# Softmax sums and reciprocals moved into earlier pairs of f tiles, and three x loads moved behind the transposes, in a fused dynamic convolution and two-matmul kernel

## The chip, the cores and the metric

The kernel runs on one core of a Trainium2 chip. The metric is the device time of one execution in microseconds (us). Ratios are the mean time of one kernel's fast runs over that of the other's fast runs of the same rounds, so they are not quite the ratio of the medians that are quoted.

Engines in the profile: PE is TensorE's matmuls, PEld its weight loads, DVE is VectorE, ACT is ScalarE, POOL is GpSimd, SP is SyncE, which issues most DMAs.

## The reference, cut to what matters

```python
def _attn_ref(x, weight_gen):                     # x (8, 4096, 192), weight_gen (8, 4096, 8, 7)
    w = softmax(weight_gen, axis=-1)              # exp, sum over 7 taps, divide
    # out[b, s, h, g] = sum over k of w[b, s, h, k] * x_pad[b, s + k, h, g]   (7 taps, causal)
    ...
def _moe_ref(x, w_in, w_out):                     # 32768 tokens, 192 -> 2048 -> 192
    h = x @ w_in
    g = h - np.tanh(h)
    return (g @ w_out).astype(np.float32)
```

## The kernel before

The 32,768 tokens are cut into 32 superblocks n of 1,024 tokens. A superblock goes through these stages:

* SyncE loads x and the tap weights. ScalarE takes the exp; VectorE takes sums, reciprocals and the scaled weights (`softmax_norm`).
* GpSimd multiplies x by the seven taps (`products`), two superblocks ahead of TensorE's use.
* TensorE adds up the taps and transposes in one go, by matmuls with an identity (`conv`); ScalarE copies the result out of PSUM (`convT`).
* TensorE's first matmul makes 16 f tiles (`gemm1`); for each, ScalarE takes the tanh and VectorE subtracts (`gt`). TensorE's second matmul (`gemm2`) runs a superblock behind, a block of tokens per pair p of f tiles.

All instructions stand in the order in which the program writes them. The parts that the change touches:

```python
psum_h = ...tile_pool(name="psum_h", bufs=3, PSUM)      # three tiles rotate: ph of gemm1, pc of conv

def softmax_norm(n, bank):
    wsm = wgpool.tile([P, J, H, K], FP32, name="wsm")
    zr_v = bank[:, 512 - J * H : 512]
    nc.vector.tensor_copy(zr_v, zr_of[n][:])            # reciprocals into PSUM, beside the transposes
    scale(nc.vector, wsm[:], e_of[n], zr_v)             # reads them there
    ...
for n in range(NTOT):
    if n + 3 < NTOT:
        load_x(n + 3)                                   # waits for GpSimd to be done with x of n + 1
    for p in range(J):
        gemm1(n, 2 * p); gemm1(n, 2 * p + 1)
        ...
        if n + 3 < NTOT:
            if p == 1:
                softmax_exp(n + 3)
            if p == 1 and n + 4 < NTOT:
                load_wg(n + 4)
            if 2 <= p <= 5:
                softmax_sum(n + 3, (p - 2) * 2, (p - 1) * 2)
            if p == 6:
                softmax_recip(n + 3, 0, J // 2)
        ...
        if p == 6 and n < NTOT - 1: break
    # the end of a superblock: "tail" below
    gemm2((n - 1) * J + 6, between=between)             # with the transposes of the third chunk mixed in
    conv(n + 1, (0, 1))                                 # the other two chunks, back to back
    gemm2((n - 1) * J + 7, 0, FILL)
    if n + 3 < NTOT:
        softmax_recip(n + 3, J // 2, J)
        softmax_norm(n + 3, pcs[0][:, 0])
    gemm1(n, NFT - 2)                                   # f tile 14
    gemm2((n - 1) * J + 7, FILL, HALF)
    gemm1(n, NFT - 1)                                   # f tile 15
    gemm2((n - 1) * J + 7, HALF, NFT)
```

Superblocks 0 to 3 add all seven taps on TensorE (seven groups of transposes). From 4 on, a DMA adds pairs of taps first, and TensorE has fewer transposes.

The softmax here doesn't subtract the row's maximum and nothing guards it: scores larger than these inputs give would overflow.

## Time and profile before

| | before |
|---|---|
| median of 4 runs | 768.27 us (767.70 to 769.29) |
| TensorE busy, profiled execution | 739.1 of 765.5 us |
| superblock in the middle (subtraction to subtraction) | 22.77 us |
| superblocks 1, 2, 3 | 28.30, 23.91, 22.97 us |

A superblock's length is read here from the start of VectorE's first subtraction of one to that of the next. "Hole" means time in which TensorE does nothing although no semaphore holds it: the profile calls its releaser "issue". The profile gives a hole as idle time after the modelled end of the last matmul; counted from record to record, as the prediction and the expectations do, it is some 0.2 us longer. Records are TensorE's instructions in the order in which they start, counted from 0, its sequencer's own included. A "fetch" is a packet of 16 KiB on the instruction queue of the trace; no view lists these singly, their times were read from the trace's DMA packets. The profile's lines themselves are shown in the prediction.

### The profile page before, as it was taken

Reading aid. Unit: us, or ns where it says so; the run is one execution under the profiler, and the core shown is the slowest. Engines: PE = TensorE matmul, PEld = TensorE weight load, DVE = VectorE, ACT = ScalarE, POOL = GpSimd, SP = SyncE. Lnnn points to the kernel's source line nnn. Section 1 sums busy time; section 2 is a strip of 40 time slices with the busy share of each in tenths; the row PEclk is TensorE's granted clock in tenths of the full one; section 3 lists DMA queues with packets and bytes.
Section 4 is the critical chain, followed back from the end, with each engine's and each line's share of the span. In section 5 each row is a group of like instructions: output and inputs, shape, how many; then the busy total and the mean of one; then the engine's idle time right before and its main releaser. Section 6 shows DMA issues by size and latency. Waiting matters only on the chain.

```text
span 765.5 us, 32560 instructions
## 1 busy us (share of the span) xinstructions
PE 739.1 (97%) x14848; PEld 564.6 (74%) x14848; DVE 681.1 (89%) x765; ACT 642.0 (84%) x869; POOL 668.9 (87%) x262
## 2 busy tenths in 40 slices
PE   4798999999999999999999999999999999999997
PEld 2476777777777777777777777777777777777777
DVE  7986899999999999999999999998999999998893
ACT  4886788888888888888888888888888888888882
POOL 8999999999999999999999999999999999999000
PEclk9999999999999999999999999999999999999999
DMA  8911467665555775545775555766555676542312
GB/s 217 236 42 57 134 171 183 182 175 121 124 151 163 182 181 117 130 150 156 182 184 129 131 144 147 182 179 151 133 131 149 173 182 169 118 122 64 81 43 85
DMA packets 25399, 110.04 MB, mean 144 GB/s; under 512 B 4671, under 2 KB 9519, under 8 KB 21294
## 3 DMA queue, kind: packets, MB, share of 16 engines
q1 hardware_dynamic: 14718, 77.03, 29.1%
q0 software_dynamic: 10544, 30.94, 25.5%
q8 instruction: 116, 1.90, 1.0%
q14 instruction: 21, 0.17, 0.1%
HBM read 54.52 MB, written 25.17 MB: 104 GB/s over the span
## 4 chain that ended last, share of the span: by engine, by line
PE 79%; DVE 15%; ACT 3%; issue 1%; DMA 1%; DVEq 0%
PE ph L308 39%; PE obank L342 37%; DVE gt L320 9%; ACT th L319 3%; DVE wsm L193 2%; PE pc L267 2%; DVE zr L163 2%; PE po L377 1%; DMA x_t<-in_x_dram 1%; DVE pc L169 1%; DVE odd L219 0%; DMA wg_t<-in_weight_gen_dram 0%; DVE even L219 0%; DVE zsum L154 0%; DVE obank L193 0%
## 5 line engine op out<-in xcount | busy, mean ns | idle before, releaser
L320 DVE TENSOR_TENSOR gt<-ph,th 128x1024 bf16<-128x1024 f32 x512 | 604.9, 1220 | 62.0 <-ACT th L319 52.8
L319 ACT ACTIVATE th<-ph 128x1024 f32<-128x1024 f32 x512 | 500.3, 1021 | 66.7 <-PE ph L308 64.8
L342 PE MATMUL obank<-w_out,gt 64*128 64x192 bf16 x7936 | 399.9, 243 | 0.8 <-ACT out_sb L361 0.4
L308 PE MATMUL ph<-convT,w_in 64*128 64x512 bf16 x3072 | 384.4, 378 | 7.9 <-DVE gt L320 2.9
L342 PEld LDWEIGHTS <-gt 64*128 64x128 bf16 x7936 | 343.6, 94 | 65.5 <-issue 0.9
L219 POOL TENSOR_TENSOR even<-x_t,wsm 128x1536 bf16<-128x1536 f32 x93 | 272.6, 2931 | 27.5 <-DVE gt L320 27.2
L219 POOL TENSOR_TENSOR odd<-x_t,wsm 128x1536 bf16<-128x1536 f32 x93 | 272.6, 2931 | 0.0
L308 PEld LDWEIGHTS <-w_in 64*128 64x128 bf16 x3072 | 163.6, 94 | 115.6 <-issue 11.7
L219 POOL TENSOR_TENSOR last<-x_t,wsm 128x1536 bf16<-128x1536 f32 x32 | 105.9, 3308 | 0.0
L361 ACT ACTIVATE out_sb<-obank 128x192 f32<-128x192 f32 x248 | 81.6, 329 | 7.0 <-PE obank L342 2.6
L291 ACT ACTIVATE convT<-pc 128x512 bf16<-128x512 f32 (+1 forms) x63 | 50.7, 807 | 30.1 <-PE pc L267 30.1
L267 PE MATMUL pc<-ident,even 64*128 64x64 bf16 x2256 | 56.1, 191 | 0.6 <-issue 0.4
L267 PEld LDWEIGHTS <-even 64*128 64x128 bf16 x2304 | 53.2, 96 | 1.4 <-issue 0.7
L234 POOL DMA_DIRECT2D even<-odd x28 | 33.7, 1205 | 8.7 <-POOL odd L219 8.7
L267 PE MATMUL pc<-ident,last 64*128 64x64 bf16 x752 | 26.8, 192 | 9.4 <-POOL last L219 9.2
L154 DVE TENSOR_REDUCE zsum<-e_t 128x16 f32<-128x112 f32 (+1 forms) x116 | 31.5, 271 | 3.0 <-ACT e_t L143 3.0
L267 PEld LDWEIGHTS <-last 64*128 64x128 bf16 x768 | 19.7, 96 | 9.7 <-POOL last L219 9.2
L143 ACT ACTIVATE e_t<-wg_t 128x448 f32<-128x448 f32 x32 | 18.5, 578 | 6.5 <-DMA wg_t<-in_weight_gen_dram 6.5
L267 PE MATMUL pc<-ident,odd 64*128 64x64 bf16 x464 | 18.5, 198 | 3.7 <-issue 2.6
L193 DVE TENSOR_TENSOR wsm<-e_t,pc 128x448 f32<-128x448 f32 x28 | 17.4, 622 | 3.1 <-DVE pc L169 0.2
L267 PEld LDWEIGHTS <-odd 64*128 64x128 bf16 x512 | 15.1, 100 | 4.6 <-issue 2.7
L163 DVE RECIPROCAL zr<-zsum 128x32 f32<-128x32 f32 (+1 forms) x58 | 16.6, 327 | 0.1
(27 smaller groups left out, 64.5 us busy)
## 6 DMA issues: line engine op xcount, KB each, us to landing
x_t<-in_x_dram SPq DMA_DIRECT2D x31, 1344.0 KB, 9.0
even<-odd POOLq DMA_DIRECT2D x28, 1024.0 KB, 8.8
out_dram<-out_sb SPq DMA_DIRECT2D x31, 768.0 KB, 11.6
wg_t<-in_weight_gen_dram SPq DMA_DIRECT2D x32, 224.0 KB, 7.8
x_t<-in_x_dram SPq DMA_DIRECT2D x1, 768.0 KB
w_out<-in_moe_w_out_dram POOLq DMA_DIRECT2D x1, 768.0 KB, 8.8
out_dram<-out_sb SPq DMA_DIRECT2D x4, 192.0 KB, 1.8
x_t<-in_x_dram SPq DMA_DIRECT2D x1, 504.0 KB
```

The source lines that it names most:

```text
L154: nc.vector.reduce_sum(out=zsum_of[n][:, j0 * H : j1 * H], in_=e_of[n][:, j0:j1].rearrange("p j h k -> p (j h) k"), axis=AX.X,)
L163: nc.vector.reciprocal(zr_of[n][:, j0 * H : j1 * H], zsum_of[n][:, j0 * H : j1 * H])
L193: return eng.tensor_mul(wsm.rearrange("p j h k -> p (j h) k"), e_t[:].rearrange("p j h k -> p (j h) k"), zr.rearrange("p (n o) -> p n o", ...
L219: mul = eng.tensor_mul(dst[k][:, :, j0:j1].rearrange("p c j h g -> p j h c g"), x_t[:, k + j0 : k + j1, :].rearrange("p j (h c g) -> p j h ...
L234: nc.gpsimd.dma_start(out=even[:].rearrange("p i c j h g -> p (i c j h g)")[:, 0:ACC], in_=odd[:].rearrange("p i c j h g -> p (i c j h g)" ...
L267: nc.tensor.matmul(pc[r][:, col : col + R] if home else pc[:, r, col : col + R], lhsT=prods[c][gi][r * R : (r + 1) * R, c, 2 * j : 2 * j + ...
L291: nc.scalar.activation(out=out, in_=pc[:, :, 0:cols].rearrange("p r (cj t) -> p r cj t", t=R), func=ACT.Copy,)
L308: nc.tensor.matmul(ph[:, r, :], lhsT=w_in[r * R : (r + 1) * R, c, f * P : (f + 1) * P], rhs=convT[r * R : (r + 1) * R, c, :], start=(c == ...
L319: last_act[0] = nc.scalar.activation(out=th[:], in_=ph_f, func=ACT.Tanh)
L320: last_sub[0] = nc.vector.tensor_sub(gt[:], ph_f, th[:])
L342: mm = nc.tensor.matmul(po[:, 0:D], lhsT=g_of[n][f][r * R : (r + 1) * R, col : col + P], rhs=w_out[r * R : (r + 1) * R, f, :], start=(r == ...
L361: last_act[0] = nc.scalar.activation(out=out_sb[:, j, :], in_=po[:, 0:D], func=ACT.Copy)
```

## The change

The intent: take the reciprocals off VectorE's row behind f tile 13, where f tile 15 waits for the product; and keep three early x loads out of the transposes.

```diff
@@ the pairs of f tiles
-                if p == 1:
+                if p == 0:
                     softmax_exp(n + 3)
-                if p == 1 and n + 4 < NTOT:
+                if p == 0 and n + 4 < NTOT:
                     load_wg(n + 4)
-                if 2 <= p <= 5:
-                    softmax_sum(n + 3, (p - 2) * 2, (p - 1) * 2)
-                if p == 6:
-                    softmax_recip(n + 3, 0, J // 2)
+                if 1 <= p <= 3:
+                    softmax_sum(n + 3, (p - 1) * 3, min(p * 3, J))
+                if 4 <= p <= 5:
+                    softmax_recip(n + 3, (p - 4) * JH, (p - 3) * JH)
@@ the tail
-            softmax_recip(n + 3, J // 2, J)
             softmax_norm(n + 3, pcs[0][:, 0])
@@ the x loads
+    LATE = (1, 2, 3)
...
-        if n + 3 < NTOT:
+        if n + 3 < NTOT and n not in LATE:
             load_x(n + 3)
...
+        if n in LATE:
+            load_x(n + 3, last_conv[0])      # behind ScalarE's copy of the transposes of n + 1
```

More of the change, by code (lines that the diff above doesn't have):

```diff
@@ L81 @@
     last_exp = {}
+    last_conv = {}
     first_halo = {}
@@ L290, in conv_out @@
             else:
-                nc.scalar.activation(
+                last_conv[0] = nc.scalar.activation(
                     out=out,
```

## The prediction

> **What bounds the kernel now.** I read the page first: engine shares, then the chain that ended last, then the costliest groups.
>
> ```profile
> PE 739.1 (97%) x14848; PEld 564.6 (74%) x14848; DVE 681.1 (89%) x765; ACT 642.0 (84%) x869; POOL 668.9 (87%) x262
> PE 79%; DVE 15%; ACT 3%; issue 1%; DMA 1%; DVEq 0%
> ```
>
> TensorE is the bound: 97% busy and 79% of the chain. Nothing that merely lightens another engine pays; only time in which TensorE stands still or runs slowly can be won. The summary of waits lists the little there is:
>
> ```profile
> PEld L308 <- DVE wsm L193: 8.5, 24, 0.5
> PE pc L267 <- issue: 3.0, 2, 2.6
> ```
>
> The first is a regular wait, 24 times some 0.35 us: first-matmul weights wait for the softmax normalisation. The second is a single hole of 2.6 us in the transposes with no wait behind it. They fit the two parts of the change, so I looked at each.
>
> *The regular wait.* VectorE's timeline at the end of a middle superblock (n = 17), columns start, length, instruction:
>
> ```profile
> 426.84 2.36 DVE L320 TENSOR_TENSOR gt<-ph,th 128x1024 bf16<-128x1024 f32 x2
> 429.12 0.56 DVE L163 RECIPROCAL zr<-zsum 128x32 f32<-128x32 f32 x2
> 429.77 0.23 DVE L169 COPY pc<-zr 128x64 f32<-128x64 f32 x1
> 430.11 0.62 DVE L193 TENSOR_TENSOR wsm<-e_t,pc 128x448 f32<-128x448 f32 x1
> ```
>
> Both reciprocals, the copy and the product stand in a row behind f tile 13. Three PSUM tiles rotate: f tile 15 takes the one that held the last transposes, and the product still reads its reciprocals there until 430.73. In the trace the matmuls ahead of f tile 15 run out so that it could start at 430.48; it starts at 430.79: 0.31 us lost.
>
> *The hole.* TensorE's timeline, and SyncE's issues near it:
>
> ```profile
> 58.82 0.22 PE L267 MATMUL pc<-ident,odd 64*128 64x64 bf16 x3
> 61.65 0.53 PE L267 MATMUL pc<-ident,odd 64*128 64x64 bf16 x13 [2.61 <-issue]
> ```
>
> ```profile
> 33.21 21.39 SPq L110 DMA_DIRECT2D x_t<-in_x_dram  x2
> 59.85 0.73 SPq L120 DMA_DIRECT2D x_t<-zero  x1
> ```
>
> TensorE stops after 3 of 16 like matmuls, so no operand is missing. The second of the two x loads merged in the first SyncE line (x of superblock 4) goes out at about 54.3 us, and the zeroing that must follow its landing is issued at 59.85. The hole lies at that load's end. Windows from f tile 13's subtraction to the next superblock's first one, for n = 1, 2 and 17 (PE, PEld, DVE, ACT, POOL busy; clock; DMA share; GB/s):
>
> ```profile
> 57.29:68.06 10.77, 8.16 (x207) 6.30 (x201) 4.98 (x8) 5.15 (x8) 10.77 (x5) 0.84 0.25 89
> 84.89:91.97 7.08, 6.69 (x203) 5.08 (x196) 4.89 (x9) 5.05 (x8) 7.08 (x3) 1.00 0.02 4
> 427.99:433.93 5.94, 5.81 (x147) 4.26 (x140) 4.98 (x8) 5.04 (x8) 5.64 (x3) 1.00 0.22 41
> ```
>
> n = 1 and 2 transpose seven groups, n = 17 fewer; yet n = 1 takes 3.7 us more than n = 2 for equal work, at a granted clock of 0.84.
>
> **What the Trainium skill says.**
> (1) "Runtime: NRT & Kernel Launch", section Instruction fetch mechanics: an engine's instructions stream in by a DMA queue in blocks of 16 KiB, 256 instructions, normally hidden. The trace agrees on the block (116 packets, 1.90 MB on the instruction queue), not on the hiding: counting TensorE's records, the hole is ahead of record 1,729 and a smaller one (0.55 us at 86.90) ahead of 2,753, just four blocks on. The block before 1,729 was begun at 56.61; the next fetch started only at 59.37, took 0.96, and TensorE resumed 1.32 after that.
> (2) "DMA: Bandwidth & Descriptors", section Queues, rings and completion order: each engine takes turns between queues packet by packet. The trace shows less fairness for this fetch: it began when the x load ended.
> (3) "TensorE: Matmul & The Clock Gate", Part 1: an idle window of some 3.4 us halves the clock. Here the hole is shorter, but the record shows half clock for 3.41 us from 61.3.
> (4) "VectorE: DVE Perf Modes", The TRN2 errata: small instructions carry a fixed cost. It agrees: sums of 112 elements take 0.26 us, of 448 take 0.62.
>
> **The change, part by part.**
> *Sums and reciprocals earlier.* Before, four sums of 2 j in pairs 2 to 5 and both reciprocals behind f tile 13. After, sums of 3, 3 and 2 j in pairs 1 to 3 and one reciprocal in each of pairs 4 and 5. The line through 0.26 and 0.62 gives 0.32 us for a sum of 3 j. A pair leaves VectorE 0.34 us from a sum's start to the next subtraction (421.27 to 421.61). Instructions overlap by about 0.08, so a sum of 3 j occupies some 0.24 to 0.27 and a reciprocal 0.26 (the second starts 0.26 after the first): all fit, with under 0.1 to spare. Behind f tile 13 the copy then starts at 429.12 and the product ends at 430.08, 0.65 earlier, ahead of 430.48: the wait of 0.31 goes.
> Not all of it is won. The next superblock's second tile needs the PSUM tile of f tile 14, whose subtraction ends at 432.47 whatever the norm does (its tanh waits for ScalarE's copy of the transposes). With release latency 0.05 it can start at 432.52, not at 432.67 - 0.31 = 432.36. So the gain is 432.67 - 432.52 = 0.15. The trace has this experiment already: superblocks 29 and 30 have no softmax left, and ScalarE's big copy of transposes comes 22.64 us after its predecessor (702.72 to 725.36), against 22.77 in the middle: 0.14. I take 25 superblocks (n = 4 to 28) x 0.14 = **3.5 us**.
>
> *Exp and the weight load a pair earlier.* ScalarE's exp (0.58) moves behind f tile 1. Its idle there is about 0.3, and its copy out moves along; I count nothing. In n = 1 two exps meet and VectorE already runs late with the ramp's sum and reciprocal (0.61 + 0.55): I charge **0.25 us**.
>
> *Late x loads.* x of 4, 5, 6 goes out behind the copy of the transposes. In n = 1 the fetch then meets a quiet DMA. Fetch to use still takes 0.1 to 0.4 + 0.95 + 1.35 = about 2.6, and the dense block lasts 2.25 (56.61 to 58.86), so 0.3 of the 2.8 us gap stays: 2.5 won. The half clock goes too: n = 1's tail is 10.77 - 7.08 = 3.7 above n = 2's, whose own hole is 0.55, so 4.2 is hole and clock together, and 4.2 - 2.8 = 1.4 is the clock. n = 2 may win 0.3, n = 3 0.1. Sum 2.5 + 1.4 + 0.4 = **4.3 us**.
> Does GpSimd starve? Its products of 4 start at 75.28; x of 4 would go out near 60.3, and land by 66 to 72 with the zeroing. x of 5: out 84, landed 93, wanted 96.5. x of 6: out 106, landed 115, wanted 118. No.
>
> **The rivals.**
> (a) *The collision moves on.* GpSimd runs back to back until 160 us and sets when the x loads of 7 and 8 go out (118.57 and 140.13), whereas TensorE arrives some 5 us earlier. In n = 4 a fetch asked for near 122 would start when x of 7 ends (124.2), usable at 126.5, wanted at 127.1: just enough. In n = 5 fetches near 140.2 and 147.9 stand against x of 8 and the output at 148.73: a hit costs 1 to 3 us. I charge **0.8 us**; all of it would bring the time to 765.
> (b) *VectorE becomes the bound.* A subtraction must end 0.05 before TensorE wants its tile, and in a pair it has 0.13. If sum or reciprocal overlapped less than I read, 5 pairs x 0.05 x 25 would cost 6 us and eat the gain (767). For it: 89% busy; against it: the ramp, where a subtraction follows a sum 0.21 after its start.
> (c) *The hole isn't the x load's fault* but the density of the transposes. Then n = 1 keeps its 2.8 us and only 3 us are won (766). For it: n = 2's hole at a DMA share of 0.02. Against it: the fetch that started 2.8 us after its block was due, as x ended.
>
> **Range and chances.** 768.7 - 3.5 - 4.3 + 0.25 + 0.8 = 761.9; I say 761.8. Without any new collision and with the holes gone altogether it would be near 760; (a) in full gives 765. So 759.5 to 765.5 for 8 in 10. Two per cent would be 15.4 us, twice the sum of all I can find idle; a loss of 2% needs a new wait of 0.9 us per superblock. Hence 0.01, 0.97, 0.02.
>
> **What would show it.** Right: the wait of weights on the softmax product gone from the list, the subtraction of f tile 14 unmoved relative to the copy, superblocks of 22.63 to 22.64; no hole near 59, no half clock at 61 to 65; x of 4 issued near 60. Wrong: issue holes in n = 4 or 5, matmuls waiting for subtractions in pairs 1 to 5, or a hole that stays at 59.

## The result

The changed kernel takes 763.66 us (median of 4, 762.46 to 765.21) against 768.27 before; the ratio is 0.994 (95% interval 0.9917 to 0.9962). By the 2% mark that is "same", and it is inside the range; but the gain is 4.6 us where 6.5 from this base (6.9 from 768.7) was predicted. The profiled execution is the fastest of the four, 762.46.

The page of the changed kernel (busy time, then the chain that ended last):

```profile
PE 737.8 (97%) x14848; PEld 575.5 (76%) x14848; DVE 676.3 (89%) x737; ACT 642.3 (84%) x869; POOL 668.7 (88%) x262
PE 93%; DVE 4%; DMA 1%; ACT 1%; issue 1%; ACTq 0%; DVEq 0%
```

VectorE's share of the chain falls from 15% to 4%: its row in the tail no longer carries it. VectorE's timeline there (n = 17; start, length, instruction):

```profile
423.16 0.34 DVE L164 RECIPROCAL zr<-zsum 128x32 f32<-128x32 f32 x1
423.50 2.36 DVE L321 TENSOR_TENSOR gt<-ph,th 128x1024 bf16<-128x1024 f32 x2
425.77 0.22 DVE L170 COPY pc<-zr 128x64 f32<-128x64 f32 x1
426.09 0.62 DVE L194 TENSOR_TENSOR wsm<-e_t,pc 128x448 f32<-128x448 f32 x1
427.90 2.38 DVE L321 TENSOR_TENSOR gt<-ph,th 128x1024 bf16<-128x1024 f32 x2 [1.18 <-ACT th L320]
```

The copy now follows the subtractions at once, and VectorE then idles for 1.18 us, because the subtraction of f tile 14 waits for its tanh. The wait of weights on the product is gone from the list of waits; in its place the list has a longer entry without a named releaser:

```profile
PEld L309 <- issue: 19.4, 54, 1.1
PE pc L268 <- issue: 1.4, 3, 0.5
PE obank L344 <- issue: 0.9, 1, 0.9
```

What was added to the first line (11.7 us in 29 times before) is the second tile of a superblock: it has 8.9 us of it in 30 times, and had 1.2 in 4. In the trace its weights start 0.055 us after the subtraction of f tile 14 ends (429.124 and 429.179), so it is this wait although the view names no releaser. The other two lines are holes. TensorE's timeline at three of them, in superblocks 1, 4 and 5:

```profile
59.96 0.36 PE L268 MATMUL pc<-ident,odd 64*128 64x64 bf16 x13 [0.54 <-issue]
...
129.67 0.71 PE L268 MATMUL pc<-ident,even 64*128 64x64 bf16 x37 [0.50 <-issue]
...
154.26 0.26 PE L344 MATMUL obank<-w_out,gt 64*128 64x192 bf16 x2 [0.91 <-issue]
```

The hole near 59 is much shorter (0.73 us from record to record, where it was 2.80) but not gone; superblocks 4 and 5 have holes that the kernel before did not have. The windows of the tails of n = 1, 2, 4, 5 and 17, with the same columns as in the prediction:

```profile
57.66:64.91 7.25, 6.68 (x202) 5.09 (x196) 4.32 (x7) 5.04 (x8) 7.25 (x4) 1.00 0.31 103
81.94:89.04 7.10, 6.68 (x202) 5.07 (x196) 4.32 (x7) 5.04 (x8) 7.10 (x3) 1.00 0.32 105
128.70:134.99 6.29, 5.77 (x142) 4.22 (x136) 4.33 (x7) 5.04 (x8) 6.29 (x3) 1.00 0.13 50
152.02:158.72 6.70, 5.79 (x145) 4.14 (x139) 4.42 (x7) 5.15 (x8) 6.40 (x4) 1.00 0.29 118
424.64:430.27 5.63, 5.63 (x143) 4.18 (x137) 4.34 (x6) 5.04 (x8) 5.33 (x3) 1.00 0.20 38
```

n = 1 falls from 10.77 to 7.25 at full clock; n = 2 keeps its length; 4 and 5 take 0.66 and 1.07 more than n = 17. The ledger of the two profiled executions:

| superblocks | before | after | won |
|---|---|---|---|
| 1 | 28.30 | 25.17 | 3.13 |
| 2 | 23.91 | 24.13 | -0.22 |
| 3 | 22.97 | 22.71 | 0.26 |
| 4 | 22.77 | 23.24 | -0.47 |
| 5 | 22.77 | 23.73 | -0.96 |
| 6 | 22.77 | 22.56 | 0.21 |
| 7 to 28 | 501.34 | 498.35 | 2.99 |
| 29 | 22.47 | 22.64 | -0.17 |

The sum is 4.8 us, which is the difference of the spans (765.5 and 760.7). The single middle superblock is 22.64 us.

### The profile page after: what moved, and what is told of

Its sections match the earlier page's. It is cut to its first block, busy times and chain, and to the rows that moved or that the text cites. A ratio compares the mean times of both kernels' runs of the same rounds, so it can differ in the third digit from the quotient of the medians.

```text
span 760.7 us, 32533 instructions
## 1 busy us (share of the span) xinstructions
PE 737.8 (97%) x14848; PEld 575.5 (76%) x14848; DVE 676.3 (89%) x737; ACT 642.3 (84%) x869; POOL 668.7 (88%) x262
## 3 DMA queue, kind: packets, MB, share of 16 engines
HBM read 54.52 MB, written 25.17 MB: 105 GB/s over the span
## 4 chain that ended last, share of the span: by engine, by line
PE 93%; DVE 4%; DMA 1%; ACT 1%; issue 1%; ACTq 0%; DVEq 0%
PE obank L344 43%; PE ph L309 43%; PE pc L268 6%; DVE gt L321 3%; PE po L379 1%; DMA x_t<-in_x_dram 1%; DVE odd L220 0%; DMA wg_t<-in_weight_gen_dram 0%; DVE even L220 0%; ACT th L320 0%; DVE zsum L155 0%; ACT e_t L144 0%; DVE zr L164 0%; DVE wsm L194 0%; ACT convT L286 0%
## 5 line engine op out<-in xcount | busy, mean ns | idle before, releaser
L309 PE MATMUL ph<-convT,w_in 64*128 64x512 bf16 x3072 | 391.3, 378 | 5.0 <-DVE gt L321 2.7
L344 PEld LDWEIGHTS <-gt 64*128 64x128 bf16 x7936 | 350.0, 94 | 59.6 <-issue 1.1
L309 PEld LDWEIGHTS <-w_in 64*128 64x128 bf16 x3072 | 172.8, 94 | 107.2 <-issue 19.4
L155 DVE TENSOR_REDUCE zsum<-e_t 128x24 f32<-128x168 f32 (+2 forms) x88 | 27.5, 312 | 3.0 <-ACT e_t L144 3.0
L164 DVE RECIPROCAL zr<-zsum 128x32 f32<-128x32 f32 (+1 forms) x58 | 20.3, 350 | 0.1
```

The costliest lines, as they stand in the source:

```text
L155: nc.vector.reduce_sum(out=zsum_of[n][:, j0 * H : j1 * H], in_=e_of[n][:, j0:j1].rearrange("p j h k -> p (j h) k"), axis=AX.X,)
L164: nc.vector.reciprocal(zr_of[n][:, j0 * H : j1 * H], zsum_of[n][:, j0 * H : j1 * H])
L309: nc.tensor.matmul(ph[:, r, :], lhsT=w_in[r * R : (r + 1) * R, c, f * P : (f + 1) * P], rhs=convT[r * R : (r + 1) * R, c, :], start=(c == ...
L344: mm = nc.tensor.matmul(po[:, 0:D], lhsT=g_of[n][f][r * R : (r + 1) * R, col : col + P], rhs=w_out[r * R : (r + 1) * R, f, :], start=(r == ...
```

## The experiments

The theory after the result: (1) the sums and reciprocals win 0.14 us per superblock and no more, because the next wait is close behind. (2) The late loads win the hole and the slow clock of superblock 1. (3) TensorE's instructions come in blocks of 256, and a hole opens where TensorE uses a block faster than the next one is fetched: because the fetch waits behind an x load, or simply because the transposes use instructions so fast. Then late loads only move the collision to the next superblock whose transposes meet a load. The rivals: the holes hang on the transposes or their data; VectorE is the bound in the pairs; the late loads carry all of the gain.

Each kernel ran in 5 rounds beside the kernel before, whose medians in the three calls were 768.59, 768.47 and 768.83 us.

### One part alone: sums_only and late_only

```diff
-    LATE = (1, 2, 3)
+    LATE = ()
```

> The changed kernel with the list of late loads empty: only the sums, reciprocals, exp and weight load moved. My theory: middle superblocks of 22.64 us as in the changed kernel (22.77 before), so some 3.3 us won there; the hole of 2.6 us near 59 us with its stretch of half clock stays, because x of superblock 4 still goes out at 54. Time about 765.0 to 765.5, if the early superblocks lose nothing more. Rival (the late loads are what carries the gain): about 768.

Measured: 766.16 us (764.45 to 766.48), ratio 0.9955 (0.9941 to 0.9969). The middle superblock is 22.64. TensorE's timeline has two large holes:

```profile
61.68 0.36 PE L268 MATMUL pc<-ident,odd 64*128 64x64 bf16 x13 [2.09 <-issue]
...
87.34 0.24 PE L268 MATMUL pc<-ident,even 64*128 64x64 bf16 x5 [2.04 <-issue]
```

The first is the known one (2.28 us from record to record). The second is larger than before (2.23 against 0.55), and here the half clock follows the second (87.82 to 91.23), not the first. So this part alone wins 0.14 us per superblock and makes superblock 2 worse, which I had not expected. TensorE arrives earlier at x of superblock 5: the block ahead of the hole begins at 82.82 instead of 84.06, and the fetch at 85.11, 2.29 after it instead of 0.43.

late_only is the kernel before with the `LATE` lines of the change.

> The kernel before with only the three late x loads. Theory: the hole at 59 shrinks from 2.6 to about 0.7 us and the half clock goes (some 3.3 us won), middle superblocks stay at 22.77; part of that is given back in superblocks 4 and 5, where TensorE now comes earlier than the x loads of 7 and 8 have drained: holes of 0.3 to 1.2 us there. Time about 765.5 to 767. Rival (the collisions at 4 and 5 need both parts): no new hole, 765.

Measured: 765.65 us median of 6, ratio 0.9972 (0.9944 to 0.9999). One of the six took 772.48 and makes the interval wide; five took 764.78 to 767.42. The middle superblock stays at 22.77. The holes from record to record: 0.60 in superblock 1, 1.11 in 2, 0.75 in 4, 0.62 in 5. The collisions in 4 and 5 therefore need only the late loads; the rival is out. Superblock 2 was worse, 1.11 against 0.55.

So each part alone wins 2 to 3 us by the medians, and both together 4.6; neither carries it all.

### Where the collision goes: late_to5

```diff
-    LATE = (1, 2, 3)
+    LATE = (1, 2, 3, 4, 5)
```

> The changed kernel with x of 7 and 8 loaded late as well (superblocks 1 to 5). Theory (the holes of 0.7 us in superblock 4 and 1.2 us in superblock 5 are instruction fetches held up by x of 7 and 8 and what queues behind them): both holes shrink to 0.4 us or less, superblocks 4 and 5 fall from 23.24 and 23.73 towards 22.7, time 1 to 1.5 us below the changed kernel (near 762.4), unless GpSimd then waits for x (wanted at 140 and 161, landing at 139 to 141 and 160 to 162), which would show as a GpSimd wait and cost TensorE nothing. Rival (the holes come from where the 256-instruction blocks end, not from the loads): holes unchanged.

Measured: 764.55 us (763.94 to 764.75), ratio 0.9941 (0.9928 to 0.9954): no gain over the changed kernel. The hole of superblock 4 is gone (none above 0.2) and that of 5 is 0.45, as the theory wants. But two new ones stand in superblocks 6 and 7:

```profile
174.72 0.19 PE L268 MATMUL pc<-ident,odd 64*128 64x64 bf16 x1 [0.37 <-issue]
...
200.47 0.41 PE L268 MATMUL pc<-ident,last 64*128 64x64 bf16 x15 [1.98 <-issue]
```

GpSimd's timeline shows why the second is so large:

```profile
166.67 2.90 POOL L220 TENSOR_TENSOR even<-x_t,wsm 128x1536 bf16<-128x1536 f32 x1 [4.79 <-DVE gt L321]
```

GpSimd stood 4.8 us ahead of superblock 8's products, longer than I expected, so x of 10 went out only at 188.33, and the fetch of the block that begins at 200.47 was 3.41 us late in starting. The subtraction that the view names had long been done (159.73). The trace shows what GpSimd waited for: x of 8, one of the late loads, begins a batch, so the zeroing of its first rows must follow it. That was issued at 159.50, but its six packets of 768 bytes moved only at 165.24 to 165.61, while GpSimd's own DMA that adds the pairs of taps was on its way (159.51 to 166.74); the semaphore that GpSimd's sequencer waited for got its last increment at 166.51. The collision moved on. My expected gain did not come.

### Where the blocks end: shift128, shift128b and shift256

Small matmuls are put ahead of the first transposes, while TensorE idles anyway. They write a PSUM tile that nothing reads; it takes one turn in the rotation of the three, in shift256 as well. Each is two instructions (weight load, matmul), so 64 of them move all later instructions by half a block, and 128 by a whole one.

```diff
+    pad = psum_h.tile([P, 2, HT], FP32, name="pad", tag="ph")
+    for _ in range(64):                                   # shift256: 128
+        nc.tensor.matmul(pad[:, 0, 0:R], lhsT=ident[0:R, :], rhs=ident[0:R, 0:R],
+                         start=True, stop=True)
     conv(0, (0, 1), (2,))
```

> The changed kernel with 64 weight loads and 64 small matmuls into an unused PSUM tile, put ahead of the first transposes while TensorE idles until 9 us: no work on the path, but every later TensorE instruction comes 128 later in its stream, half a block. Theory (a block of 256 instructions is fetched only when the one two before it is used up, so a hole opens where one block is used faster than the 2.9 us that a fetch takes): the holes of 0.73 and 0.58 us in superblocks 1 and 2 go, since there no block lies wholly in dense transposes; time 1 to 2 us below the changed kernel, with holes at other records, each still at a multiple of 256 plus 193. Rival (the holes hang on the transposes or on data): same holes at the same transposes, same time.

Measured: four executions took 762.31 to 763.58 us (ratio 0.992, 0.9906 to 0.9934), but the profiled one took 1,983.28 us and is no use for the holes: TensorE was busy 99% of it, every matmul stretched (832 ns against 378 for the first matmul, 455 against 243 for the second), and the trace has no record of the granted clock. It was not seen again in the other kernels' executions, and its cause stays open.

> The kernel with 64 small matmuls ahead of the first transposes once more: in its first call four executions took 762.3 to 763.6, but the profiled one took 1983 us with every matmul stretched, so its trace tells nothing of the holes. Theory: no hole above 0.3 us in superblocks 1 and 2; what holes there are stand at a record of 193 plus a multiple of 256, now half a block earlier in the kernel's text; about 1 us below the changed kernel of this call. Rival: holes at the same transposes as in the changed kernel.

Measured: 762.05 us (761.72 to 763.25), ratio 0.9922 (0.9908 to 0.9935), against 763.97 and 0.9944 for the changed kernel in the same call. The tails of superblocks 1 and 2 take 6.54 us each (7.25 and 7.10 in the changed kernel): their holes are gone. Only one hole above 0.25 us is left, in superblock 4:

```profile
131.89 0.51 PE L344 MATMUL obank<-w_out,gt 64*128 64x192 bf16 x8 [1.84 <-issue]
```

It stands at TensorE's record 4,801, which is 193 plus 18 x 256, and no longer in the transposes but in the second matmul.

> The changed kernel with 128 small matmuls (256 instructions, one whole block) ahead of the first transposes: as much idle time filled as with 64 and more, but the ends of the blocks fall on the same transposes as without them. Theory (where the blocks end decides): the holes of some 0.7 and 0.6 us in superblocks 1 and 2 are back, at records 1,985 and 3,009, and those of superblocks 4 and 5 too; time as the changed kernel, 763 to 764.5. Rival (the early matmuls help in another way, by warming the clock or by delaying something): no holes in 1 and 2, time near 762.

Measured: 764.40 us (761.72 to 767.50), ratio 0.9936 (0.9915 to 0.9957). The holes are back at the very transposes where the changed kernel has them:

```profile
60.39 0.36 PE L268 MATMUL pc<-ident,odd 64*128 64x64 bf16 x13 [0.89 <-issue]
...
84.69 0.24 PE L268 MATMUL pc<-ident,even 64*128 64x64 bf16 x5 [0.69 <-issue]
```

From record to record they are 1.07 and 0.88 us, even longer than in the changed kernel (0.73 and 0.58): the fetches took 1.40 and 1.22 us here, 0.96 and 0.99 there. Their records are 1,985 and 3,009, and those of superblocks 4 and 5 are 4,801 and 5,825, each one block later than in the changed kernel. As much idle time was filled as with 64 matmuls and more, so it is the place of the block ends that counts. This decides for the instruction blocks. Over 13 profiles (before, after, and all but shift128's stretched one), 46 instructions of TensorE from record 449 on start more than 0.41 us after the one before without waiting for a semaphore, and all 46 stand at a record of 193 plus a multiple of 256. (The limit is just above the 0.40 us of a first matmul at the half clock.) The fetches fit too: all 46 start 1.19 to 1.58 us after a fetch has ended, however late that fetch began (0.06 to 4.55 us after the block before).

### What the fetch waits for: after_x4 and sums_x4, with after_again

```diff
-            dma = rows(0, P)
-            if behind is not None:
-                order(dma, behind, "order of the loads")
+            for r0, r1 in ((0, 4), (4, 8), (8, 11), (11, 14)):
+                dma = rows(0, P, r0, r1)
+                if behind is not None:
+                    order(dma, behind, "order of the loads")
```

after_again is the changed kernel as it is.

> The changed kernel once more, as the measure for the three others of this call. Theory and rival alike: 763 to 764; its holes of about 0.7, 0.6, 0.7 and 1.2 us in superblocks 1, 2, 4 and 5 again, within a few tenths (how far the fetches are held up varies from run to run).

Measured: 763.97 us (762.84 to 765.40), ratio 0.9944 (0.9932 to 0.9957). The holes in its profiled execution (765.40, the slowest of the five) are 0.72, 0.58, 1.11 and 1.97: the first two repeat, those in superblocks 4 and 5 vary by 0.4 and 0.8 from the first profile (0.69 and 1.15). That is much of the spread between executions.

> The changed kernel with each x load issued as four loads of 3 or 4 of its 14 rows. In the profile of the kernel before, the fetch that was late began 0.01 us after the last descriptor of the x load had gone through: 8 descriptors of 10,752 bytes for each DMA engine, one after the other. Theory (an engine finishes the descriptors of one load before it turns to the fetch): with pieces of a quarter, a fetch waits about 1 us instead of 3, so the holes in superblocks 4 and 5 fall below 0.4 us, those of 0.7 and 0.6 in superblocks 1 and 2, which no load causes, stay; time 1 to 1.5 us below the changed kernel. Rival (the fetch waits for everything queued, or for the bandwidth): holes of 4 and 5 unchanged.

Measured: 762.79 us (761.87 to 763.28), ratio 0.9925 (0.9912 to 0.9937). The time is about 1.2 us below the changed kernel, though the intervals overlap a little, and not for the expected reason: its profile (763.28, the slowest of the five) has a hole of 1.92 in superblock 4, a larger one than after_again's. Only that of 5 is small (0.28).

> The changed kernel without its late loads, with each x load in four pieces. Theory: the holes of 2.3 us in superblocks 1 and 2, which the same kernel with whole x loads showed, shrink to about 1 us, and no half clock follows; time near 763.5, so that splitting the load does what delaying it does. Rival (only keeping the load out of the transposes helps): holes above 2 us, time near 766.

Measured: 763.91 us (763.62 to 765.06), ratio 0.9943 (0.9931 to 0.9956).

```profile
61.48 0.36 PE L269 MATMUL pc<-ident,odd 64*128 64x64 bf16 x13 [2.18 <-issue]
```

Superblocks 1 and 2 have holes of 2.37 and 1.90 us, as with whole loads (2.28 and 2.23): **my theory of one load's descriptors is wrong**. In superblock 2 the fetch began at 84.36, after the last packets of x (83.35) and of the tap weights (83.92) and among those of an output (82.40 to 85.77), all issued by 78.9; the smaller loads did not let it in between. What a fetch waits for is not settled by this: in the kernel before, one began at 124.16, with only 48 of the 128 packets of an x load through, and the trace doesn't say which DMA engine moved a packet. That sums_x4 is still some 2 us faster than sums_only fits its clock: no half clock followed its holes. I don't know why, and the two kernels ran on different chips.

### Whether VectorE has room: lumped and one_back

lumped takes the sum in one piece in pair 1 and the reciprocal in one piece in pair 4; one_back leaves the first reciprocal in pair 4 and puts the second behind f tile 13 again.

```diff
 # lumped
-                if 1 <= p <= 3:
-                    softmax_sum(n + 3, (p - 1) * 3, min(p * 3, J))
-                if 4 <= p <= 5:
-                    softmax_recip(n + 3, (p - 4) * JH, (p - 3) * JH)
+                if p == 1:
+                    softmax_sum(n + 3)
+                if p == 4:
+                    softmax_recip(n + 3)
 # one_back
-                if 4 <= p <= 5:
-                    softmax_recip(n + 3, (p - 4) * JH, (p - 3) * JH)
+                if p == 4:
+                    softmax_recip(n + 3, 0, JH)
 ...
+            softmax_recip(n + 3, JH, J)
             softmax_norm(n + 3, pcs[0][:, 0])
```

> The changed kernel with one sum of all 8 j in pair 1 and one reciprocal of 64 in pair 4, instead of three sums and two reciprocals. Theory (VectorE has room for 0.34 us in a pair and TensorE's tile wants the subtraction 0.08 us later at most; sum and reciprocal take 0.54 and 0.47 there): TensorE waits twice in a superblock, 0.05 to 0.12 us each, middle superblocks of 22.8 to 22.9 instead of 22.64, time 4 to 6 us above the changed kernel. Rival (VectorE is off the path in the pairs): 22.64 and no loss.

Measured: 768.06 us (767.66 to 768.44), ratio 0.9987 (0.9975 to 0.9999). The middle superblock is 22.74, so 0.10 us of the 0.14 is lost. VectorE's timeline at the one sum:

```profile
416.65 0.61 DVE L155 TENSOR_REDUCE zsum<-e_t 128x64 f32<-128x448 f32 x1
417.18 4.79 DVE L321 TENSOR_TENSOR gt<-ph,th 128x1024 bf16<-128x1024 f32 x4
```

The sum holds VectorE for 0.53 us, more than a pair's 0.34, and the next two pairs run without a pause until it has caught up. Without room, VectorE does bound the pairs; in pieces it doesn't. The pieces are needed. Some 2.5 us of this are the 25 superblocks; the rest (about 1.5 us) are larger holes in superblocks 4 and 5 of this profile (1.84 and 2.16).

> The changed kernel with the second reciprocal put back behind f tile 13, the first left in pair 4. Theory (the product must only end before TensorE reaches f tile 15; with no reciprocal it ends some 0.4 us early, with one some 0.1 early): middle superblocks stay at 22.64, time as the changed kernel. Rival (each reciprocal taken out of the row is worth half of the gain): 22.70, 1.7 us above it.

Measured: 764.86 us median of 6, ratio 0.9941 (0.9917 to 0.9964), with a wide spread (761.34 to 767.09) that the holes of superblocks 4 and 5 (1.40 and 2.23 in the profile) and a late start may explain. The middle superblock, which is what the run was for, is 22.64: one reciprocal in the tail costs nothing. VectorE's timeline:

```profile
429.49 0.34 DVE L164 RECIPROCAL zr<-zsum 128x32 f32<-128x32 f32 x1
429.94 0.23 DVE L170 COPY pc<-zr 128x64 f32<-128x64 f32 x1
430.27 0.62 DVE L194 TENSOR_TENSOR wsm<-e_t,pc 128x448 f32<-128x448 f32 x1
```

The product ends 1.40 us after the reciprocal's start, instead of 1.61 with two (429.12 to 430.73 in the kernel before), so 0.21 earlier and not 0.4 as I had put it: f tile 15 still waits some 0.1 us. The tail shows it (5.73 from f tile 13's subtraction to the next superblock, against 5.63 in the changed kernel), but the next superblock's pairs take 16.90 instead of 17.00: the second tile, which waits for f tile 14 anyway, takes the 0.1 up. The gain is a threshold, not a sum over instructions.

### The best of them

shift128 with `LATE = (1, 2, 3, 4)`.

> The changed kernel with 64 small matmuls ahead and x of superblock 7 late too. With 64 matmuls and three late loads the only large hole left was 2.2 us in superblock 4, under x of 7 and what queues behind it. Theory: it goes; no hole above 0.5 us anywhere; 2 us below that kernel, near 760. Rival (the collision moves on to the next superblock again, as it did when x of 7 and 8 both went late): a hole of 1 us or more in superblocks 5 to 7, time near 762.

Measured: 762.11 us (761.23 to 762.88), ratio 0.991 (0.9897 to 0.9922). The hole of 2.2 us in superblock 4 is gone; holes of 0.48, 1.17 and 0.65 stand in superblocks 2, 6 and 13, the largest here:

```profile
175.61 0.27 PE L268 MATMUL pc<-ident,last 64*128 64x64 bf16 x7 [0.98 <-issue]
```

So it went halfway: the expected 760 did not come, and the collision moved to superblock 6, smaller than before. Its ratio is the lowest of all, 6.7 us below the kernel before by the medians; but its interval overlaps that of shift128b. They were run at other times.

## Why the prediction was right, and where its sum was off

**The bound and the regular wait: right, in size too.** The product's wait went, and the subtraction of f tile 14 stayed where it was: it ended 3.20 us after ScalarE's big copy began, in both traces (429.27 to 432.47 before, 425.93 to 429.12 after). Superblocks of 22.63 to 22.64 were foretold, and 22.64 came. 25 superblocks at 0.14 is 3.5; the ledger has 3.0 for 22 of them. That superblocks 29 and 30 already showed the answer before anything was built was the best reading in the prediction.

**The late loads: mechanism right, size 0.9 us too large.** The half clock near 61 us went as foretold, the hole shrank, and GpSimd did not starve. Superblocks 1 to 3 won 3.17 us together, where 4.3 less 0.25 was predicted. The step that failed is "Fetch to use still takes 0.1 to 0.4 + 0.95 + 1.35 = about 2.6". In the changed kernel, with the DMA quiet, it was 0.61 + 0.96 + 1.41 = 2.98 in superblock 1 and 0.42 + 0.99 + 1.46 = 2.87 in superblock 2. So 0.73 of the hole stayed instead of 0.3, and superblock 2 won nothing: its hole of 0.55 had never been the load's. There rival (c), density of the transposes, was the truth, and I had noted the sign for it (a DMA share of 0.02) and passed over it. Half a block of shift removed both, which settles it. The ramp's charge of 0.25 was also small: superblock 1 took 0.39 us longer up to f tile 13. The prediction's point (2), that the fetch began when the x load ended, holds for the hole near 59 and not for fetches in general, as 124.16 below shows.

**Rival (a): it happened, and cost twice the charge.** 0.8 us was charged; superblocks 4 and 5 lost some 1.4 in the ledger, 1.7 with the 0.14 that each should have won. Their holes are 0.69 and 1.15 in one profile, 1.11 and 1.97 in the other. In superblock 4 the step "a fetch asked for near 122 would start when x of 7 ends (124.2)" failed twice over. TensorE was only some 3 us ahead, not 5, and the block whose start asks for it began at 124.11. And x of 7 does not end at 124.2: in the kernel before that is when a fetch began, in the middle of the load, whose packets moved from 122.26 to 128.29. In the changed kernel they moved from 122.38 to 128.06, and the fetch began at 127.21, with 123 of the 128 through. The load had been issued at 118.61; its first packet moved when those of GpSimd's DMA were nearly through (they ended at 123.32). In superblock 5 the first profile has another cause: the fetch began in time (150.96, 0.36 after its block), but took 2.11 us, beside the packets of tap weights and an output (150.89 to 155.73); in after_again it began 2.09 late.

**Rival (b): avoided, as argued.** VectorE's room of 0.34 us in a pair is real: lumped lost 0.10 us per superblock by passing it.

**The sum.** The ledger is 2.0 us short of the predicted 6.75: 0.9 in superblocks 1 to 3, 0.9 in 4 and 5, and nearly all of the rest in superblock 29, which lost 0.17. The time came inside the range because the range had left room for (a) in full. Two of the prediction's own signs of being wrong came, the holes in superblocks 4 and 5 and, a quarter as long, the one near 59; the third, matmuls waiting for subtractions in the pairs, did not.

## What to carry to other kernels

When a wait is taken away, find the next one on the same engine before counting the gain: here 0.31 us of waiting was worth 0.14, and a single instruction less in the row was enough. Where an engine stops with no semaphore, count its instructions: holes at a fixed distance of records were instruction fetches here, and they depended on how densely instructions were used, on the DMA traffic at the time, and on where blocks happened to end, which a few instructions in idle time can move. Moving a load out of one dense stretch is worth checking against the next one, since a faster engine meets the following loads earlier.

## What the Trainium skill lacked or had wrong

* "Runtime: NRT & Kernel Launch", section Instruction fetch mechanics, has the block of 256 instructions right and calls its cost mostly hidden. Here it was not: the largest hole was 2.8 us, and even with the DMA quiet the way from a block's start to the use of the next took 2.9 to 3.0 us in the changed kernel (waiting 0.4 to 0.6, the fetch 1.0, then 1.4 to 1.5 until TensorE ran), so a block used faster than that stalls. The page gives no such figure. That a fetch is asked for when the block before begins is my reading of the traces, not a recorded event; in the kernel before, 18 of the 116 fetches began ahead of that, by up to 1.12 us.
* "DMA: Bandwidth & Descriptors", section Queues, rings and completion order, has an engine take turns between queues packet by packet, and calls 9 to 17 descriptors a typical packet. Whether that fails here stays open. The fetch of 59.37 started as the x load ended (last write at 59.36), but this load has 128 packets of 10,752 bytes, 8 for each of 16 engines if shared evenly, so a turn could take in all of them. x in four pieces didn't shorten the wait (holes of 2.37 and 1.90 against 2.28 and 2.23), which speaks against turns by packet; the fetch that began amid a load (124.16) speaks for them.
* "TensorE: Matmul & The Clock Gate", Part 1, ties the half clock to an idle window of about 3.4 us. Holes of 2.2 to 2.8 us sometimes brought it here (before, superblock 1; sums_only, superblock 2) and sometimes not (sums_only, superblock 1; sums_x4, both).
* No page tells of a whole execution like the one of 1,983.28 us, with matmuls 1.9 to 2.2 times as long, superblocks of 61.0 us and no record of the granted clock; it came once and its cause is open.
